# An attention and MLP kernel whose output split, normalising engine and early value loads were changed, together with one number of its planner

## The chip, the cores and the metric

One core of one Trainium2 chip. The metric is device microseconds of that core for one execution of the program. Ratios are computed as the mean time of one kernel's fast runs over the mean of the other's fast runs of the same rounds on the same chip, so they are not quite the ratios of the medians that are quoted.

## The reference

Eight batches of eight heads, 576 queries, 16 "beacon" keys in front of 576 ordinary ones, 64 wide; then an MLP over all 4,608 tokens.

```python
k_all = np.concatenate([beacon_k, k], axis=2)
v_all = np.concatenate([beacon_v, v], axis=2)
scores = np.matmul(q, k_all.transpose(0, 1, 3, 2)) / np.sqrt(D)   # causal for the ordinary keys
a = softmax(scores)
attn = np.matmul(a, v_all)                     # -> x [4608, 512]
h = x @ w_in                                   # 512 -> 2048
out = (h * sigmoid(1.702 * h)) @ w_out         # 2048 -> 512
```

## The kernel before

Attention runs in 32 steps (eight batches, four head pairs each). One step is: scores (TensorE, s<-qT,kT), exp (ScalarE, E<-s), masks on the diagonal blocks (GpSimd or VectorE, E<-E), outputs (TensorE, u<-E,vb), evictions (O<-u), and a normalisation on VectorE: two transposes that bring the sums of the exps together (zt<-O), a reciprocal, a transpose back (rz<-rt), two multiplications (xT<-O,rz). The MLP (u<-xT,w and u<-w,g) is cut into nine groups of 512 tokens and woven in between.

No instruction stands where a person put it. Each piece of work is an object with an estimated duration, an allowed engine or two, and a priority. A greedy planner runs once, while the program is built, and takes at each turn the piece that could start first by its estimates. The order that comes out is the fixed order of each engine's instructions.

```python
class Work:                     # eng: one engine with dur, or a dict of engines with their durations
    def __init__(self, eng, dur, key, fn, needs=(), alloc=None, dma=0.0, mode=0, after=()): ...
# --- cut ---
    zn.append(Work(
        "DVE", 0.68, i + 0.48, lambda i=i, x=x: z_turn(i, x), evs[-2:],   # 0.68 us: the estimate for zt<-O
        alloc=zb[0] if not zn else None, after=zn[:1],
    ))
# --- cut ---
    nw = Work(
        dict(DVE=0.78, POOL=1.42), 0, i + 0.45, lambda eng, i=i, x=x: norm(i, x, eng),
        [zk], alloc=xTb[b] if p + x == 0 else None, ...
    )
# --- cut ---
def issue():
    # --- cut ---
    # each turn: of all work whose needs are placed, the one with the smallest (start by estimate, mode, key)
    eng = min(w.opts, key=lambda e: max(t, free[e]) + w.opts[e] + ...)
    t = max(t, free[eng])
    c = (t, 0 if w.mode == mode == 1 else 1, w.key)
    # --- cut ---
order = issue()
for w in order:
    w.fn(w.eng) if w.flex else w.fn()
```

The outputs of a head are made in two parts of 288 queries, from nine matmuls. For batches 0 and 1 the values come in rows of 1,536 B and are spread to their partitions by matmuls with a constant matrix; from batch 2 on they are loaded straight to their rows.

```python
HS = S // 2
def av_list(x, half):
    qa, qe = half * HS, (half + 1) * HS
    return [(j, lo - qa, hi - qa, col) for j in range(NJ)
            for (lo, hi, col) in e_pieces(j, max(qa, s0s[j]), qe)]
# --- cut ---
def v_pe(b, j):                  # batches 0 and 1
    # --- cut: the beacons' values, by one matmul with the identity ---
    for t in range(TR):
        nc.tensor.matmul(u[:, :].rearrange("r (h d) -> r h d", h=H),
                         spread[:, j * P - t + TR : (j + 1) * P - t + TR], v6(b)[:, :, t, :], ...)
```

The softmax here doesn't subtract the row's maximum and nothing guards it: scores larger than these inputs give would overflow.

## Time and profile before

| | before |
|---|---|
| time, median of 7 runs beside the last experiments | 397.91 us |
| span of the profiled run | 395.7 us |
| TensorE, VectorE, GpSimd busy | 368.3, 259.0, 189.1 us |
| first MLP matmul | 47.49 us |
| four batch stages (exp table load to exp table load, 107.72 to 278.36 us) | 43.39, 41.80, 43.07, 42.38: 170.64 us |

ScalarE loads the exp table again after each group of gelus (seven loads of 1.28 us on the page), so these loads mark one batch's stage well, and two kernels can be compared stage by stage. The page's lines and the stage table are in the prediction. One more view was needed later: TensorE's own order in one of these stages (151.11 to 192.91 us; start, duration, what, how many; in brackets the wait in front and what ended it).

```profile
154.54 3.63 PE L512 MATMUL u<-w,g 128*128 128x512 f16 x16
158.10 0.60 PE L351 MATMUL s<-qT,kT 64*128 64x512 f16 x8
158.63 1.62 PE L421 MATMUL u<-E,vb 128*128 128x288 f16 x18
160.18 0.61 PE L351 MATMUL s<-qT,kT 64*128 64x464 f16 x4
160.72 3.63 PE L512 MATMUL u<-w,g 128*128 128x512 f16 x16
164.28 0.60 PE L351 MATMUL s<-qT,kT 64*128 64x512 f16 x8
164.81 1.62 PE L421 MATMUL u<-E,vb 128*128 128x288 f16 x18
166.36 0.37 PE L351 MATMUL s<-qT,kT 64*128 64x464 f16 x2
166.66 3.63 PE L512 MATMUL u<-w,g 128*128 128x512 f16 x16
170.22 0.48 PE L351 MATMUL s<-qT,kT 64*128 64x208 f16 x4
170.63 0.40 PE L421 MATMUL u<-E,vb 128*128 128x288 f16 x3
171.10 0.39 PE L351 MATMUL s<-qT,kT 64*128 64x64 f16 x6
172.01 0.37 PE L351 MATMUL s<-qT,kT 64*128 64x464 f16 x2 [0.53 <-ACT E L364]
172.32 0.54 PE L421 MATMUL u<-E,vb 128*128 128x224 f16 x4
174.19 1.01 PE L421 MATMUL u<-E,vb 128*128 128x208 f16 x11 [1.33 <-POOL E L387]
```

Twice there is a regular pattern: a w2 block of 16 matmuls (3.6 us), eight score matmuls, a whole step's 18 outputs, four score matmuls of 464 and 208 columns that feed the next step's last exps. The third time only two of those four stand in front of the w2 block. The other two come behind it, so that step's last exps and masks are no longer hidden under the block, the outputs are cut in pieces, and TensorE waits for a mask. I call this the broken third step.

### The profile page before, as it was taken

The numbers are of one execution on the slowest core, as the hardware profiler recorded it, in microseconds if no ns is written. First come the engines' busy times: TensorE is split into PE (matmuls) and PEld (weight loads), VectorE is DVE, ScalarE is ACT, GpSimd is POOL, SyncE is SP. The second block draws the span as 40 slices with busy tenths as digits, with TensorE's granted clock in tenths as the row PEclk, the third lists the DMA queues.
The fourth block names the chain that finished last, engine by engine and source line by source line (L and its number), as shares of the span: only waits on it lengthen the run. The fifth ranks groups of instructions, "written<-read, shape, count | busy, mean of one in ns | idle before, by whom it ended". The sixth has DMA issues, their size and how long they took to land.

```text
span 395.7 us, 6410 instructions
## 1 busy us (share of the span) xinstructions
PE 368.3 (93%) x2458; PEld 186.3 (47%) x2458; DVE 259.0 (65%) x425; ACT 227.3 (57%) x333; POOL 189.1 (48%) x282
## 2 busy tenths in 40 slices
PE   6997999989999799979997999979999999999996
PEld 3464544444544344534453774435454544444442
DVE  6469998699739973999469963997485349000021
ACT  1788766457674656656744766466658563644400
POOL 8664853469255854478337925584355044000000
PEclk9999999999999899999999899999999999999999
DMA  8999994849562795379346966279310010001022
GB/s 114 200 206 208 145 128 132 210 97 154 116 164 60 157 115 132 86 172 124 110 113 145 134 108 146 67 148 120 110 54 30 0 55 27 28 0 53 2 80 80
DMA packets 60894, 42.81 MB, mean 108 GB/s; under 512 B 32192, under 2 KB 53184, under 8 KB 60864
## 3 DMA queue, kind: packets, MB, share of 16 engines
q0 software_dynamic: 42816, 18.62, 38.8%
q1 hardware_dynamic: 18048, 23.79, 18.9%
q8 instruction: 19, 0.31, 0.3%
q14 instruction: 11, 0.09, 0.1%
HBM read 44.40 MB, written 16.61 MB: 154 GB/s over the span
## 4 chain that ended last, share of the span: by engine, by line
PE 50%; DVE 21%; DMA 5%; ACT 4%; issue 2%; POOL 2%; POOLq 1%; DVEq 0%; ACTq 0%
PE u L490 29%; PE u L512 13%; DMA n<-in_k_dram 5%; PE u L421 5%; DVE zt L444 4%; DVE O L432 4%; DVE xT L463 4%; DVE sq L275 4%; PE s L351 2%; ACT E L364 2%; ACT L364 2%; DVE rz L454 2%; DVE t L284 2%; POOL xT L463 1%; POOL t L284 1%
## 5 line engine op out<-in xcount | busy, mean ns | idle before, releaser
L490 PE MATMUL u<-xT,w 128*128 128x512 f16 (+1 forms) x640 | 133.7, 361 | 3.9 <-DVE O L432 1.6
L364 ACT ACTIVATE E<-s 128x1024 f16<-128x1024 f32 (+3 forms) x128 | 104.6, 873 | 49.2 <-PE s L351 45.5
L512 PE MATMUL u<-w,g 128*128 128x512 f16 x576 | 129.4, 379 | 2.3 <-DVE O L432 2.1
L502 ACT ACTIVATE g<-u 128x512 f16<-128x512 f32 x144 | 85.1, 597 | 59.6 <-PE u L490 59.3
L490 PEld LDWEIGHTS <-w 128*128 128x128 f16 x640 | 60.4, 99 | 62.7 <-issue 8.3
L512 PEld LDWEIGHTS <-g 128*128 128x128 f16 x576 | 54.8, 98 | 67.5 <-issue 3.4
L387 POOL TENSOR_SCALAR_AFFINE_SELECT E<-E 128x256 f16<-128x256 f16 (+2 forms) x144 | 58.6, 425 | 42.1 <-ACT E L364 40.8
L463 POOL TENSOR_TENSOR xT<-O,rz 64x576 f16<-64x576 f32 x24 | 40.8, 1701 | 71.6 <-DVE rz L454 71.5
L525 DVE COPY osb<-u 128x512 f32<-128x512 f32 x26 | 17.7, 681 | 76.9 <-PE u L512 76.8
L421 PE MATMUL u<-E,vb 128*128 128x288 f16 (+6 forms) x576 | 58.2, 246 | 7.8 <-POOL E L387 5.7
L432 DVE COPY O<-u 128x288 f32<-128x288 f32 x109 | 45.8, 442 | 27.0 <-PE u L421 26.5
L421 PEld LDWEIGHTS <-vb 128*128 128x128 f16 (+1 forms) x576 | 44.0, 98 | 25.6 <-issue 14.6
L444 DVE STREAM_TRANSPOSE zt<-O 64x576 f32<-64x576 f32 x64 | 49.4, 772 | 1.9
L463 DVE TENSOR_TENSOR xT<-O,rz 64x576 f16<-64x576 f32 x40 | 48.8, 1220 | 0.7
L351 PE MATMUL s<-qT,kT 64*128 64x80 f16 (+5 forms) x384 | 39.9, 286 | 6.1 <-ACT E L364 4.6
L284 POOL COPY t<-sq 128x576 f16<-128x576 f16 x22 | 30.7, 1397 | 26.6 <-DVE sq L275 26.6
L275 DVE STREAM_TRANSPOSE sq<-n 128x576 f16<-128x576 f16 x48 | 35.7, 755 | 4.4 <-DMA n<-in_k_dram 3.8
L351 PEld LDWEIGHTS <-kT 64*128 64x128 f16 x384 | 14.5, 94 | 32.6 <-issue 26.5
L454 DVE STREAM_TRANSPOSE rz<-rt 128x576 f32<-128x576 f32 x32 | 24.4, 762 | 1.3 <-DVE t L290 0.4
L243 POOL DMA_DIRECT2D vb<-in_v_dram x24 | 20.8, 873 | 0.0
L284 DVE COPY t<-sq 128x576 f16<-128x576 f16 x26 | 19.7, 757 | 0.5
L523 ACT COPY osb<-u 128x512 f32<-128x512 f32 x10 | 5.9, 588 | 17.0 <-PE u L512 17.0
(50 smaller groups left out, 147.0 us busy)
## 6 DMA issues: line engine op xcount, KB each, us to landing
out_dram<-osb SPq DMA_DIRECT2D x36, 256.0 KB
d<-t SPq DMA_DIRECT2D x24, 148.0 KB
kT<-d SPq DMA_DIRECT2D x12, 296.0 KB
n<-in_k_dram POOLq DMA_DIRECT2D x12, 288.0 KB, 5.3
n<-in_q_dram POOLq DMA_DIRECT2D x12, 288.0 KB, 6.2
d<-t SPq DMA_DIRECT2D x24, 144.0 KB
qT<-d SPq DMA_DIRECT2D x12, 288.0 KB
vb<-in_v_dram POOLq DMA_DIRECT2D x18, 128.0 KB, 5.5
```

Of the source, the lines that this page charges most:

```text
L275: nc.vector.transpose(sqs[(b, g, w)][:, c * n : (c + 1) * n, :, :], nat[(b, g, w)][:, c * n : (c + 1) * n, :],)
L284: copy[eng](out=tqk[(b, g, w)][:, e, o : o + S].rearrange("p (r t) -> p r t", t=TPP), in_=sqs[(b, g, w)][:, :, e, :].rearrange("p t r -> p ...
L351: nc.tensor.matmul(sc[:, x, o : o + e - a], kT[r : r + 64, p, j * P : (j + 1) * P], qT[r : r + 64, p, a:e], start=True, stop=True,)
L364: nc.scalar.activation(out=Es[i][:, :, choff[ci] : choff[ci] + w], in_=scs[(i, ci)][:, :, 0:w], func=AFT.Exp, scale=0.125,)
L387: nc.gpsimd.affine_select(out=blk, in_=blk, compare_op=ALU.is_ge, fill=0.0, base=mc, pattern=[[0, 2], [1, w]], channel_multiplier=-1,)
L421: nc.tensor.matmul(u[:, lo:hi], vb[0:kw, j, :, :].rearrange("r h c -> r (h c)")[:, o : o + 2 * D], E[0:kw, x, col : col + hi - lo], start= ...
L432: copy[eng](out=Os[i][:, x, half * HS : (half + 1) * HS], in_=avu[(i, x, half)][:, :])
L444: nc.vector.transpose(zst[i][0][64 * x : 64 * x + 64, :, :], Os[i][64 * (1 - x) : 64 * (1 - x) + 64, x, :])
L463: vec[eng].tensor_tensor(out=xT[r : r + 64, p, c : c + S], in0=Os[i][r : r + 64, x, :], in1=zst[i][2][r : r + 64, :], op=ALU.mult,)
L490: nc.tensor.matmul(u[:, o : o + w], w1t[:, kp, nt * P : (nt + 1) * P], xT[:, kp, m : m + w], start=(kp == 0), stop=(kp == NKP - 1),)
L502: nc.scalar.activation(out=gts[g][:, nt, :], in_=hu[(g, nt)][:, :], func=AFT.Gelu_apprx_sigmoid)
L512: nc.tensor.matmul(o[:, :], gts[g][:, nt, mt * P : (mt + 1) * P], w2t[:, nt, :], start=(nt == 0), stop=(nt == NNT - 1),)
```

## The change

Its stated intent: split the outputs at query 240, where a key block begins, and merge neighbouring pieces (seven matmuls a head for nine); normalise on VectorE only; load the second batch's values straight to their rows, behind w1. With that come an earlier mask constant, the second weight placed behind the next q and k, per-batch buffer names, and one planner estimate: 0.68 became 0.74.

```diff
-    HS = S // 2
+    HS = 2 * P - Nb
+    AQ = (0, HS, S)
+    NBV = 1
 # --- cut: u tile and evictions by AQ ---
-            if lo < hi:
+            if lo < hi and got and got[-1][1] == lo and got[-1][2] + lo - got[-1][0] == col + lo - qa:
+                got[-1] = (got[-1][0], hi, got[-1][2])
+            elif lo < hi:
                 got.append((lo, hi, col + lo - qa))
 # --- cut: rings qT0, qT1, kT0, kT1, vb0, vb1 of one buffer each for qT, kT, vb of two ---
-    mkeep = Work("POOL", 0.3, 0.0, make_keep)
+    mkeep = Work("POOL", 0.3, -4.75, make_keep)
 # --- cut: spread matmuls only for b < NBV; bk loads no longer wait for batch 1's values ---
-                "POOL", 0.9 + 0.6 * (j == 0), 4 * b - 1.5 + 0.1 * j,
+                "POOL", 0.9 + 0.6 * (j == 0), (4 * b - 1.5 if b >= NB2 else -3.9) + 0.1 * j,
                 lambda b=b, j=j: load_v(b, j, 0, H),
-            [vpe[NJ - 1], vpe[2 * NJ - 1]][c > 0 :][:1] if c < 3 else [], dma=3.0,
+            vpe[-1:] if 2 * c < 3 * NBV else [], dma=3.0,
+            after=[Lq[(2, 1, 0)]],
-                "DVE", 0.68, i + 0.48, lambda i=i, x=x: z_turn(i, x), evs[-2:],
+                "DVE", 0.74, i + 0.48, lambda i=i, x=x: z_turn(i, x), evs[-2:],
-                dict(DVE=0.78, POOL=1.42), 0, i + 0.45, lambda eng, i=i, x=x: norm(i, x, eng),
+                dict(DVE=0.78), 0, i + 0.45, lambda eng, i=i, x=x: norm(i, x, eng),
```

More of the change, by code (lines that the diff above doesn't have):

```diff
@@ L81 @@
     bkn = cst.tile([Nb, NB2, H, D], F16, tag="bkn", name="bkn")
-    bvn = cst.tile([Nb, NB2, H, D], F16, tag="bvn", name="bvn")
+    bvn = cst.tile([Nb, NBV, H, D], F16, tag="bvn", name="bvn")
     def make_keep():
@@ L166, in load_beacons @@
             out=t.rearrange("n b h d -> n (b h) d"),
-            in_=src[0:NB2].rearrange("b h n d -> n (b h) d"),
+            in_=src[0 : t.shape[1]].rearrange("b h n d -> n (b h) d"),
         )
@@ L401, in av_list @@
     def av_list(x, half):
-        qa, qe = half * HS, (half + 1) * HS
+        qa, qe = AQ[half : half + 2]
         return [
@@ L413, in av_half @@
         E = Es[i]
-        u = psu.tile([P, HS], F32, tag="u", name="u")
+        u = psu.tile([P, AQ[half + 1] - AQ[half]], F32, tag="u", name="u")
         avu[(i, x, half)] = u
@@ L432, in av_out @@
         copy[eng](
-            out=Os[i][:, x, half * HS : (half + 1) * HS], in_=avu[(i, x, half)][:, :]
+            out=Os[i][:, x, AQ[half] : AQ[half + 1]], in_=avu[(i, x, half)][:, :]
         )
@@ L552 @@
     rings = dict(
-        n0=2, n1=2, sq=2, t0=2, t1=2, d0=4, d1=4, qT=2, kT=2, vb=2, s=2, E=2, u=4, O=3,
+        n0=2, n1=2, sq=2, t0=2, t1=2, d0=4, d1=4, qT0=1, qT1=1, kT0=1, kT1=1, vb0=1, vb1=1, s=2, E=2, u=4, O=3,
         zt=2, rt=2, rz=2, xT=RING, g=2, osb=3,
@@ L586, in first_loads @@
                     ))
-        lv = Work("POOL", 0.8, kl + 0.2, lambda b=b: load_v6(b), dma=3.6)
-        fb = []
         ub = Buf("u")
@@ L610, in first_loads, with first_values @@
         pk[b] = y
+    def first_values(b):
+        lv = Work("POOL", 0.8, -4.8, lambda b=b: load_v6(b), dma=3.6)
         for j in range(NJ):
@@ L613, in first_loads @@
             kk = 4 * b + 0.5
-            x = Work("PE", 1.35, kk, lambda b=b, j=j: v_pe(b, j), [lv, mspread] + beac[1:], alloc=ub, after=vpe[-1:])
+            x = Work("PE", 1.35, kk, lambda b=b, j=j: v_pe(b, j), [lv, mspread] + beac[1:], alloc=ub,
+                after=vpe[-1:],
+            )
             V[(b, j)] = Work(
@@ L624 @@
     for b in range(B):
-        kTb[b], qTb[b], vbb[b], xTb[b] = Buf("kT"), Buf("qT"), Buf("vb"), Buf("xT")
+        kTb[b], qTb[b], vbb[b] = (Buf(f"{n}{b % 2}") for n in ("kT", "qT", "vb"))
+        xTb[b] = Buf("xT")
         bt = [qTb[b], kTb[b]]
@@ L628 @@
             first_loads(b)
-            continue
-        for g in range(2):
+        for g in range(2) if b >= NB2 else ():
             for w in (1, 0):
@@ L659 @@
                         bkB = [
-                            Work("POOL", 0.6, 4.3, lambda x=x: load_bk(x), [V[1, 0]], dma=0.7)
+                            Work("POOL", 0.6, 4.3, lambda x=x: load_bk(x), after=[ld_], dma=0.7)
                             for x in range(HG)
@@ L681 @@
                 placed[(b, g, w)] = pl
+        if b < NBV:
+            first_values(b)
+            continue
         for j in range(NJ):
             V[(b, j)] = Work(
-                "POOL", 0.9 + 0.6 * (j == 0), 4 * b - 1.5 + 0.1 * j,
+                "POOL", 0.9 + 0.6 * (j == 0), (4 * b - 1.5 if b >= NB2 else -3.9) + 0.1 * j,
                 lambda b=b, j=j: load_v(b, j, 0, H),
```

## The prediction

> **What bounds the kernel now.** I read the page's busy table first, then the chain that ended last, then one table of busy time by stage (cut at the moments where a gelu group begins or ends), then TensorE's own waits, and last the engines' order of instructions in the first 65 us and from 107 to 135 us.
>
> The page's first part, busy us and share of the span, and its line of the chain by engine:
>
> ```profile
> PE 368.3 (93%) x2458; PEld 186.3 (47%) x2458; DVE 259.0 (65%) x425; ACT 227.3 (57%) x333; POOL 189.1 (48%) x282
> ...
> PE 50%; DVE 21%; DMA 5%; ACT 4%; issue 2%; POOL 2%; POOLq 1%; DVEq 0%; ACTq 0%
> ```
>
> TensorE is busy 93% and carries half of the chain. VectorE carries 21% though it is busy only 65%, so it binds in some stages. By stage (span of the stage, then busy us of TensorE, its weight loads, VectorE, ScalarE and GpSimd, each with its number of instructions, then granted clock, DMA share, GB/s):
>
> ```profile
> 22.97:47.49 24.52, 21.65 (x233) 12.83 (x229) 23.31 (x40) 20.16 (x34) 15.82 (x33) 1.00 1.23 188
> 47.49:107.00 59.51, 55.64 (x367) 27.44 (x364) 52.30 (x85) 36.82 (x55) 32.81 (x42) 1.00 0.78 138
> 107.00:151.00 44.00, 41.05 (x253) 19.89 (x252) 33.61 (x56) 26.71 (x38) 25.03 (x35) 0.96 0.65 125
> 151.00:193.00 42.00, 39.41 (x251) 19.05 (x250) 33.18 (x55) 26.41 (x39) 25.02 (x35) 1.00 0.69 131
> 193.00:236.00 43.00, 40.60 (x313) 25.92 (x312) 32.91 (x54) 26.17 (x38) 25.02 (x35) 0.96 0.65 118
> 236.00:278.00 42.00, 38.88 (x248) 18.88 (x247) 32.58 (x54) 25.86 (x37) 25.01 (x35) 1.00 0.67 123
> 278.00:335.00 57.00, 56.75 (x363) 28.11 (x362) 34.17 (x60) 35.15 (x50) 22.35 (x36) 1.00 0.13 46
> 335.00:395.70 60.70, 55.62 (x257) 24.94 (x255) 6.84 (x10) 19.11 (x32) 1.90 (x1) 0.99 0.11 39
> ```
>
> From the first value (22.97 us, first attention output) to the first MLP matmul (47.49 us) VectorE is busy 23.31 of 24.52 us: that stage is VectorE's. The four batch stages of 42 to 44 us are TensorE's, with 2.4 to 3.1 us of gaps each. In two of them the clock is 0.96: 0.04 x 43 us is another 1.7 us each. From 278 us on there is almost nothing to win but one wait of 1.2 us for a GpSimd normalisation. The pool of lost TensorE time from 47 us to 278 us is so 3.9 + 2.95 + 2.6 + 2.4 + 3.1 + 2 x 1.7, about 18 us.
>
> Two groups that the change touches (busy us, mean ns):
>
> ```profile
> L463 DVE TENSOR_TENSOR xT<-O,rz 64x576 f16<-64x576 f32 x40 | 48.8, 1220 | 0.7
> L463 POOL TENSOR_TENSOR xT<-O,rz 64x576 f16<-64x576 f32 x24 | 40.8, 1701 | 71.6 <-DVE rz L454 71.5
> L214 PE MATMUL u<-w,spread 96*128 96x512 f16 x60 | 13.5, 380 | 0.0
> ```
>
> And what a batch stage's gap hangs on (GpSimd's order, start and duration):
>
> ```profile
> 108.83 1.90 POOL L463 TENSOR_TENSOR xT<-O,rz 64x576 f16<-64x576 f32 x1 [5.51 <-DVE rz L454]
> 110.81 0.38 POOL L387 TENSOR_SCALAR_AFFINE_SELECT E<-E 128x224 f16<-128x224 f16 x1
> 111.13 0.62 POOL L131 DMA_DIRECT2D n<-in_k_dram  x1
> ```
>
> GpSimd sat 5.51 us in front of a normalisation, and the mask and the next k load queued behind it. VectorE's transposes of that k began only at 116.98 us, after 1.48 us of waiting for it, and from there VectorE was full to 144 us, with a TensorE gap of 1.46 us at 130.3.
>
> [...]the normalisation has two SBUF inputs, takes 719 ns at best and up to 2519 ns on VectorE, and its mean is 1220 ns while GpSimd does 24 of the 64. [...]The trace has 18 attention matmuls with 3,328 columns[...] in 1.55 us[...]. [...]A row of v is 64 values, 256 B in HBM, and the page lists 32192 of 60894 packets under 512 B[...]. [...]here a gap of 1.46 us at 130 us already went with a granted clock of 0.67 over 130 to 135 us[...].
>
> **The change part by part.**
>
> *Split at 240.* Per head the pieces were 288, 176, 48 and 224, 64, 288, 288, 208, 80: nine. Key blocks begin at queries 0, 112, 240, 368 and 496, and the block at 240 no longer reaches into the first part; the 224 and 64 lie side by side and merge. New: 240, 128 and 336, 336, 336, 208, 80: seven, with the same 1,664 columns. 128 matmuls and weight loads go. [...]I take 0.8 us. Evictions keep their columns. The first part now needs only two masks, which helps latency.
>
> *Second batch's values.* Goes: 30 matmuls at 216 ns and one with the identity, 6.7 us of TensorE (it ran 36.97 to 44.4 us), four evictions of 0.58 us on ScalarE and one of 0.69 us on VectorE, and one 576 KB load. Comes: six loads, issues of 0.55, 0.84 and 4 x 0.90 us, 5.0 us of GpSimd; the same bytes in 256 B rows. Elsewhere such a batch of v was issued at 90.3 to 96.1 us and the queues calmed at about 100 us, so about 10 us of the queue, against 3 us (0.59 MB written at the 200 GB/s of this stage): 7 us more, in a stage where DMA is busy until 57 us. The 6.7 us are not all won, since VectorE binds there: from 23.9 us to the last normalisation of the first batch at 44.03 us it has hardly a gap. TensorE is held up by the removed work only from there to 47.49 us. So the MLP can start at about 44 us, 3.5 us sooner; if the values land too late for step 4's output to have run before it, 1.6 us of that is only postponed. I take 2.5 us.
>
> *Early mask constant, second weight behind the next q and k.* The constant was ready at 18.2 us, with VectorE waiting 4.5 us for it; now VectorE can mask the first steps while GpSimd issues loads. No gain in itself, since the first output waits for the first batch's values until 22.2 us; it protects against the longer GpSimd queue.
>
> *Normalising on VectorE.* GpSimd loses 40.8 us. VectorE gains 24 instructions. Without a partner two in a row took 1.49 to 1.63 us (28.8 to 42.5 us), 0.78 each; with some blocking by GpSimd's remaining copies I take 0.85: 64 x 0.85 = 54.4 against 48.8, +5.6 us. GpSimd, being freer, will take some of VectorE's 26 reordering copies (0.757 us each); six of them give 4.5 us back. VectorE's sum hardly changes. What is won is order: masks and k loads no longer stand behind a normalisation. At 110 us the k load could go 0.6 us sooner, and VectorE could begin up to 1.2 us sooner. A quarter of the 18 us pool, with the clock, is 4.5 us; the wait of 1.2 us near the end shrinks by 0.4. I take 4.6 us for both.
>
> *Buffer names* change only the order of allocation. Sum: 0.8 + 2.5 + 4.6 = 7.9 us; 397.88 - 7.9 = 390.0 us.
>
> **The rivals.** (a) TensorE's sum is all that counts: 6.7 + 0.8 us come off, and the gaps shrink too. For it: 93% busy, MLP work can fill any gap. Against: the removed 6.7 us lie in VectorE's stage. It gives 386 us. (b) The new loads hurt. GpSimd's ninth open load waited for the first to land: issue 10 waited for 2, issue 15 for 7, issue 16 for 8. If eight may be open, the last value loads wait for w1, whose issues take 16.7 us to land, and the masks behind them wait until about 28 us; the second weight, last issued at 46.9 us before and needed at 65.9, could land late as well and open a gap before the second MLP matmul. That gives back 3 to 5 us: 393 to 395. (c) VectorE becomes the bound in the batch stages: they hold 33 of 42 us of it. With 5.6 us spread over eight batches and bursts already full, gaps grow by 0.5 us each: 394 us. (d) Nothing in the middle moves, because k loads are gated by an exp (109.01 to 110.04 us) and not by the normalisation; then 397.88 - 3.3 = 394.6 us.
>
> **Range and chances.** Line of 2%: 389.9 us, just where I land. (a) and a fuller start pull down to 384, (b) to (d) up to 396. The schedule is rebuilt as a whole from estimates, so a step may miss by a few us either way. Faster by over 2%: 0.47; within 2%: 0.49; slower: 0.04.
>
> **What would show it.** The identity and spread matmuls number 31, not 62; attention matmuls 448; GpSimd has no normalisation and the 64 on VectorE average 0.75 to 0.95 us. The first MLP matmul starts at 43 to 45.5 us; if it is at 47 or later, the start's step is wrong. Gaps and lost clock from there to the end of the last batch stage fall from about 18 to about 13 us; if they stay, (d) holds, and if they grow with VectorE full, (c). A gap before the first w2 matmul, or masks in the first 30 us held up behind value loads, shows (b). A kernel at 386 or below would say that removed TensorE work counts in full.

## The result, and the profile after

The changed kernel takes 386.65 us (385.37 to 387.29, four runs) against 397.99; the ratio is 0.9706, 95% interval 0.9671 to 0.9741: faster. The time lies inside the predicted range of 384 to 396 us, 3.35 us below its estimate of 390.0. The stages tell another story than the prediction's sum, though.

| stage | before | after | difference |
|---|---|---|---|
| to the first MLP matmul | 47.49 | 51.21 | +3.72 |
| first gelu group (to 65.97 / 67.27) | 18.48 | 16.06 | -2.42 |
| first stage (to 107.72 / 109.41) | 41.75 | 42.14 | +0.39 |
| four batch stages | 170.64 | 157.82 | -12.82 |
| the rest | 117.34 | 116.37 | -0.97 |
| span | 395.7 | 383.6 | -12.1 |

The start got worse, where 2.5 us were to be won. The four batch stages gave all the gain, in columns as in the prediction's stage table:

```profile
109.41:149.29 39.88, 38.91 (x233) 18.52 (x232) 33.54 (x57) 25.90 (x37) 19.22 (x32) 1.00 0.72 138
149.29:188.52 39.23, 38.88 (x234) 18.43 (x232) 33.59 (x58) 25.79 (x37) 18.82 (x32) 1.00 0.74 135
188.52:228.00 39.48, 39.04 (x297) 24.73 (x296) 33.21 (x58) 25.82 (x37) 19.33 (x32) 1.00 0.76 135
228.00:267.23 39.23, 38.88 (x233) 18.41 (x232) 33.60 (x58) 25.79 (x37) 18.75 (x32) 1.00 0.75 134
```

TensorE is busy 38.9 of 39.2 us and the clock is 1.00: a stage without gaps. GpSimd has 6 us less, VectorE no less than before. The normalisation group, all on VectorE now:

```profile
L467 DVE TENSOR_TENSOR xT<-O,rz 64x576 f16<-64x576 f32 x64 | 52.2, 816 | 0.9
```

The start has lines that answer to the prediction's rival (b). GpSimd's order (start, duration, what, and the wait in front):

```profile
23.93 0.88 POOL L245 DMA_DIRECT2D vb<-in_v_dram  x1 [1.68 <-DMA w<-in_moe_w_in_dram]
26.43 0.73 POOL L245 DMA_DIRECT2D vb<-in_v_dram  x1 [1.62 <-DMA w<-in_moe_w_in_dram]
27.16 1.73 POOL L391 TENSOR_SCALAR_AFFINE_SELECT E<-E 128x256 f16<-128x256 f16 x5
```

TensorE's order at the same place:

```profile
28.26 2.73 PE L425 MATMUL u<-E,vb 128*128 128x128 f16 x13 [3.46 <-POOL E L391]
```

Two stretches of 2 us, with the granted clock third from the end:

```profile
26.00:28.00 2.00, 0.00 (x0) 0.00 (x0) 0.00 (x0) 0.00 (x0) 1.57 (x4) 0.73 1.24 206
36.00:38.00 2.00, 2.00 (x11) 0.87 (x10) 1.97 (x4) 1.84 (x4) 2.00 (x4) 0.50 1.09 158
```

The last value loads wait for w1 to land, the masks of step 1 stand behind them, TensorE stands still for 3.46 us, and its clock is then at half (0.50) until about 41 us. That is rival (b), and dearer than it was priced.

The first stage has one more gap, in front of the first w2 matmul. The two score matmuls there stand behind an exp for which ScalarE first finishes its gelus (the last starts at 66.65 us) and loads a table (1.28 us from 67.27 us):

```profile
69.64 0.37 PE L355 MATMUL s<-qT,kT 64*128 64x464 f16 x2 [3.02 <-ACT E L368]
69.94 3.63 PE L516 MATMUL u<-w,g 128*128 128x512 f16 x16
```

The second weight is not what is late: its four loads, issued from 43.1 us on, took 14.4 us at most to land. This gap of 3.02 us is in the traces of all six kernels below that have the values' part, and in none of the other eight.

### The profile page after: what moved, and what is told of

It is laid out like the page before. It is cut to its first block, busy times and chain, and to the rows that moved or that the text cites.

```text
span 383.6 us, 6063 instructions
## 1 busy us (share of the span) xinstructions
PE 363.8 (95%) x2299; PEld 180.3 (47%) x2299; DVE 264.4 (69%) x446; ACT 226.2 (59%) x334; POOL 149.0 (39%) x260
## 4 chain that ended last, share of the span: by engine, by line
PE 69%; DMA 11%; ACT 8%; DVE 7%; issue 2%; POOL 2%; SPq 0%; ACTq 0%; POOLq 0%; DVEq 0%
PE u L494 28%; PE u L516 24%; PE u L425 11%; PE s L355 6%; ACT E L368 5%; DMA w<-in_moe_w_in_dram 4%; DMA d<-t 3%; ACT L368 2%; DVE zt L448 2%; DVE O L436 2%; DMA n<-in_k_dram 2%; DVE xT L467 1%; DMA g<-in_q_dram 1%; DMA qT<-d 1%; DVE sq L277 1%
## 5 line engine op out<-in xcount | busy, mean ns | idle before, releaser
L506 ACT ACTIVATE g<-u 128x512 f16<-128x512 f32 x144 | 83.8, 598 | 51.4 <-PE u L494 51.2
L529 DVE COPY osb<-u 128x512 f32<-128x512 f32 x29 | 19.6, 675 | 76.1 <-PE u L516 76.0
L425 PE MATMUL u<-E,vb 128*128 128x336 f16 (+4 forms) x448 | 59.4, 277 | 3.5 <-POOL E L391 3.5
L436 DVE COPY O<-u 128x240 f32<-128x240 f32 (+1 forms) x103 | 42.4, 432 | 20.1 <-PE u L425 18.6
L467 DVE TENSOR_TENSOR xT<-O,rz 64x576 f16<-64x576 f32 x64 | 52.2, 816 | 0.9
L425 PEld LDWEIGHTS <-vb 128*128 128x128 f16 (+1 forms) x448 | 39.7, 101 | 26.0 <-issue 9.0
L355 PE MATMUL s<-qT,kT 64*128 64x80 f16 (+5 forms) x384 | 40.8, 293 | 7.5 <-ACT E L368 6.3
L286 POOL COPY t<-sq 128x576 f16<-128x576 f16 x24 | 28.7, 1196 | 32.3 <-DVE sq L277 31.8
L286 DVE COPY t<-sq 128x576 f16<-128x576 f16 x24 | 26.6, 1108 | 0.2
L245 POOL DMA_DIRECT2D vb<-in_v_dram x28 | 24.5, 881 | 5.7 <-DMA w<-in_moe_w_in_dram 3.3
L436 ACT COPY O<-u 128x336 f32<-128x336 f32 (+1 forms) x25 | 10.3, 428 | 7.7 <-PE u L425 7.7
```

The source lines that it names most:

```text
L286: copy[eng](out=tqk[(b, g, w)][:, e, o : o + S].rearrange("p (r t) -> p r t", t=TPP), in_=sqs[(b, g, w)][:, :, e, :].rearrange("p t r -> p ...
L355: nc.tensor.matmul(sc[:, x, o : o + e - a], kT[r : r + 64, p, j * P : (j + 1) * P], qT[r : r + 64, p, a:e], start=True, stop=True,)
L425: nc.tensor.matmul(u[:, lo:hi], vb[0:kw, j, :, :].rearrange("r h c -> r (h c)")[:, o : o + 2 * D], E[0:kw, x, col : col + hi - lo], start= ...
L436: copy[eng](out=Os[i][:, x, AQ[half] : AQ[half + 1]], in_=avu[(i, x, half)][:, :])
L467: vec[eng].tensor_tensor(out=xT[r : r + 64, p, c : c + S], in0=Os[i][r : r + 64, x, :], in1=zst[i][2][r : r + 64, :], op=ALU.mult,)
L506: nc.scalar.activation(out=gts[g][:, nt, :], in_=hu[(g, nt)][:, :], func=AFT.Gelu_apprx_sigmoid)
```

## The experiments

The questions: which part removes the gaps of the batch stages, and what delays the start? Twelve kernels ran, all correct. The columns "figure" to "values" say what of the change a kernel has; "stages" is the sum of the four batch stages, "rest" the span from the first MLP matmul on.

| run | figure | norm. on VectorE | split 240 | values | first MLP | stages | rest | ratio to before |
|---|---|---|---|---|---|---|---|---|
| before | 0.68 | | | | 47.49 | 170.64 | 348.2 | 1 |
| b1_norm_dve | 0.68 | yes | | | 47.74 | 164.85 | 343.9 | 0.9927 |
| b2_norm_flip | 0.68 | in place | | | 47.60 | 165.45 | 342.1 | 0.9849 |
| b3_split240 | 0.68 | | yes | | 47.52 | 169.39 | 345.1 | 0.9921 |
| b4_values | 0.68 | | | yes | 51.89 | 167.91 | 347.6 | 1.0085 |
| c1_norm_split | 0.68 | yes | yes | | 47.97 | 164.40 | 341.6 | 0.9853 |
| e2_after_z68 | 0.68 | yes | yes | yes | 52.67 | 166.84 | 343.5 | 1.0030 |
| e1_z_only | 0.74 | | | | 49.63 | 158.82 | 334.2 | 0.9692 |
| c2_norm_split_z | 0.74 | yes | yes | | 47.09 | 158.02 | 332.5 | 0.9615 |
| c3_norm_values | 0.74 | yes | | yes | 50.15 | 158.82 | 337.1 | 0.9752 |
| the changed kernel | 0.74 | yes | yes | yes | 51.21 | 157.82 | 332.4 | 0.9706 |
| d1_late_values | 0.74 | yes | yes | later | 48.97 | 157.53 | 332.1 | 0.9669 |
| d2_later_values | 0.74 | yes | yes | later still | 49.20 | 157.08 | 335.8 | 0.9743 |
| e3_z78 | 0.78 | yes | yes | | 48.80 | 158.67 | 334.3 | 0.9646 |

**The parts one by one.** My theory after the result was that GpSimd's queue had been in the way and the normalisations' move had cleared it. The rivals were the split and the values.

b1_norm_dve, normalisations on VectorE alone:

```diff
-                dict(DVE=0.78, POOL=1.42), 0, i + 0.45, ...
+                dict(DVE=0.78), 0, i + 0.45, ...
```

> The kernel before with one edit: normalisations may only go to VectorE (the plan is made anew). Theory N (the batch stages are gap-free in the changed kernel because GpSimd's in-order queue no longer stands behind a normalisation): the four stages from one exp table load to the next between 107 and 278 us fall from 43.4, 41.8, 43.1, 42.4 us to 40 to 41 us (the changed kernel has 39.9, 39.2, 39.5, 39.2), the clock is 1.00 in them, and the whole takes 0.97 to 0.98 of before (386 to 391 us); the start is unchanged. Rival S (the split at 240 does it): ratio 0.995 to 1.005 and the stages stay at 42 to 43. Rival V (the values' new load shifts the plan): as S.

Measured: 0.9927 (0.9895 to 0.9959), stages of 41.2 us each. The stages lost 5.8 us of 170.6, not 12.8, and the first stage grew from 41.75 to 44.70 us, so the whole moved only 0.7%. The theory holds for less than half of the gain.

b2_norm_flip keeps the plan of the kernel before in every place and only issues the 24 GpSimd normalisations on VectorE:

```diff
-        w.fn(w.eng) if w.flex else w.fn()
+        w.fn("DVE" if 1.42 in w.opts.values() else w.eng) if w.flex else w.fn()
```

> The kernel before with its plan kept in every place: the order is the one computed with both engines allowed, but each of the 24 normalisations planned for GpSimd is issued on VectorE at its place. Theory N says it is GpSimd's queue and not a new plan: stages of 40 to 41.5 us, ratio 0.97 to 0.985. If only the new plan helps, ratio 0.99 to 1.01.

Measured: 0.9849 (0.982 to 0.9879), at the edge of theory N's range, with stages of 40.8 to 42.2 us, two of them above its 41.5. The same move with the old order is worth 1.5%, with a newly computed plan 0.7%. So replanning itself moves the time by as much as a part of the change does.

b3_split240, the split and the merging alone:

```diff
-    HS = S // 2
+    HS = 2 * P - Nb
+    AQ = (0, HS, S)            # and the merging of pieces, as in the change
```

> The kernel before with only the split at query 240 and the merged pieces. Theory N: attention matmuls 448 for 576, about 1 us off: ratio 0.995 to 1.0, stages 41.5 to 43. Rival S: stages 39.5 to 40.5 us, ratio 0.97 to 0.98.

Measured: 0.9921 (0.9889 to 0.9953), a little more than expected; 1.3 us of it in the first stage (40.42 for 41.75 us) and as much in the four batch stages together. Rival S is out: the batch stages stay at about 42 us.

b4_values has the change with its normalisation, split and figure undone:

```diff
 # the changed kernel, with
-    HS = 2 * P - Nb
+    HS = S // 2                # and no merging
-                "DVE", 0.74, i + 0.48, ...
+                "DVE", 0.68, i + 0.48, ...
-                dict(DVE=0.78), 0, i + 0.45, ...
+                dict(DVE=0.78, POOL=1.42), 0, i + 0.45, ...
```

> The kernel before with only the part for the second batch's values (their loads, the order of the weight loads and the masks' constant, the buffers' names). Theory: the first MLP matmul comes later than 47.5 us, at about 51, because mask instructions stand behind value loads that wait for w1; TensorE loses 6.7 us of work; ratio 0.99 to 1.01. Rival V: the batch stages fall to 40 us and the ratio is 0.975 to 0.985.

Measured: 1.0085 (1.0051 to 1.0118), slower, though within 2%; first MLP matmul at 51.89 us, as expected. The batch stages stay at 41.7 to 42.3 us, so rival V is out. Taking 31 matmuls off TensorE, with all that came with it, made the kernel slower. No part alone comes near 0.9706, and their effects taken together (-0.7 or -1.5, -0.8 and +0.9%) would give -0.6 to -1.4%.

**The parts together.** c1_norm_split joins b1 and b3; c2_norm_split_z is c1 with one number changed:

```diff
-                "DVE", 0.68, i + 0.48, lambda i=i, x=x: z_turn(i, x), evs[-2:],
+                "DVE", 0.74, i + 0.48, lambda i=i, x=x: z_turn(i, x), evs[-2:],
```

> The kernel before with two parts: normalisation on VectorE only, and the split at 240 with merged pieces; the second batch's values stay as they were. Alone the two gave 0.993 and 0.992. Theory P (only both together leave the batch stages without gaps: with the normalisations moved alone, TensorE still waited 8.2 us for output evictions on VectorE): stages of 39.2 to 39.8 us, first MLP matmul at 47.5 us, ratio 0.962 to 0.970, so faster than the changed kernel, whose start is 4 us later. Rival A (the parts just add): ratio 0.985, stages of 40.5 us, and the values' part is needed for the rest.

> As the run before it, and with the plan's figure for the sum's transpose at 0.74 instead of 0.68 us, as in the changed kernel. Theory P: within 0.3% of the run before it, stages 39.2 to 39.8 us. Rival Z (that planning figure is what removes the gaps): this one 0.962 to 0.970 and the run before it 0.98 or more.

Measured: c1 0.9853 (0.981 to 0.9896) with stages of 41.1 us, c2 0.9615 (0.9566 to 0.9664) with three stages of 39.2 us and one of 40.3. Theory P fell and rival Z, which I had put in only because the line stood in the diff, won. (c1's ratio is also that of rival A, by which the parts just add; but A needs the values' part for the rest of the gain, and c2 has the rest without it.) An estimate of a duration was worth 2.4%, and c2 at 382.28 us is the fastest kernel measured; its interval just misses the changed kernel's (0.9671 to 0.9741), which was measured in other rounds. TensorE's waits in c1 and in c2 (in total us, times, longest):

```profile
PE u L493 <- DVE O L435: 7.7, 5, 1.6
```

```profile
PE u L493 <- DVE O L435: 0.9, 5, 0.3
```

The evictions in front of the MLP matmuls came in time in c2, though the instructions are nearly the same ones and VectorE is busy no less (264.37 for 263.48 us).

c3_norm_values is the changed kernel with the split undone (`HS = S // 2`, no merging).

> The changed kernel with the split put back to 288 and the pieces unmerged (normalisation and values' part kept). Theory P: the gaps of the batch stages come back to 41 us each, first MLP matmul at 51 us, ratio 0.990 to 1.0. If the values' part is what interacts with the normalisation, ratio 0.97 to 0.975.

Measured: 0.9752 (0.9703 to 0.9802), stages of 39.2 to 40.3 us: theory P fell here too. The other half of the expectation names a cause, values with normalisation, that is not needed either, as e1 shows below. The changed kernel, with the split, is 0.5% faster (0.9752 against 0.9706, intervals overlapping), mainly in the first stage (45.20 against 42.14 us). That difference is one of clock: behind the same gap of 3.02 us the w2 block of 16 matmuls took 6.34 us here and 3.63 us in the changed kernel, and the clock of the first stage was 0.92 here and 1.00 there. So it is not shown to be the split's.

d1_late_values asks about the start: the second batch's value loads wait, in the plan, for step 1's first exp, so that four masks come before them.

```diff
+    for j in range(NJ):
+        late.append((V[(1, j)], 1))
```

> The changed kernel, but in the plan the second batch's value loads wait for the first exp of step 1, so that four of that step's mask instructions stand in front of them on GpSimd. Theory M (the late start of the MLP comes from masks behind loads that may not be issued until w1 has landed): the gap of 3.46 us before 28.26 us goes, the second step's output runs at about 25 us, the first MLP matmul comes at 46.5 to 49 us for 51.2, and the ratio to before is 0.960 to 0.967 (0.9706 without it). Rival D (the data itself, 256 B rows in a full queue, comes late): first MLP matmul stays at 50 us or later and the ratio at 0.970 or above.

Measured: 0.9669 (0.962 to 0.9717), first MLP matmul at 48.97 us; the wait of 3.46 us became two of 1.33 and 1.57. This agrees with theory M, but the interval overlaps the changed kernel's.

**The figure.** e1_z_only changes nothing in the kernel before but 0.68 to 0.74; e2_after_z68 puts 0.68 back in the changed kernel.

> The kernel before with one number changed: the planner's duration for the sum's transpose is 0.74 us for 0.68 (the trace has 0.772). No instruction is added or taken away, only the order may differ. Theory Z (this figure is the main part of the gain by itself): ratio 0.97 to 0.98, batch stages 39.5 to 41 us. Theory NZ (it needs the normalisations on VectorE, as a plan in which both fit): ratio 0.99 to 1.005, stages 42 us.

> The changed kernel with only that number put back to 0.68. Both Z and NZ: the batch stages go back to about 41 us each, ratio to before 0.985 to 0.995 (0.9706 with 0.74). If the stages stay at 39.2 us, the figure mattered only without the values' part.

Measured: e1 0.9692 (0.9645 to 0.974), e2 1.003 (0.9973 to 1.0088). The number alone gives what the whole change gives, and the whole change without it gives nothing; e2 is slower than either theory had expected, since what its batch stages gain (3.8 us) its start loses (5.2 us). e1 still has 24 normalisations on GpSimd, nine matmuls a head and the spread values, and three of its stages take 39.29 us. The first of them, in the stage table's columns:

```profile
107.69:146.98 39.29, 38.72 (x249) 19.01 (x248) 32.86 (x58) 25.52 (x36) 22.81 (x33) 1.00 0.73 136
```

And TensorE's order in its second stage:

```profile
162.24 0.60 PE L351 MATMUL s<-qT,kT 64*128 64x464 f16 x4
162.77 3.63 PE L512 MATMUL u<-w,g 128*128 128x512 f16 x16
166.33 0.60 PE L351 MATMUL s<-qT,kT 64*128 64x512 f16 x8
166.86 1.62 PE L421 MATMUL u<-E,vb 128*128 128x288 f16 x18
```

In front of the third w2 block there are now four score matmuls for the two of before, and the third step's 18 outputs run whole, without a wait. The traces show the same in all four batch stages of all fourteen kernels of the table: with 0.68 (seven kernels, 28 stages) the third step is always broken in this way, and with 0.74 or 0.78 (seven kernels, 28 stages) it is always whole. With a broken step the normalisations' place matters (42.7 us a stage before, 41.2 in b1, as means of the four); with a whole one it does not (39.7 in e1 and in c3). Of the 2.51 us by which the kernel before's second stage is longer than e1's, 2.03 us are gaps of TensorE (2.59 for 0.56), and 1.86 us of these stand inside the broken step (0.53 and 1.33).

ScalarE's order shows where the plans part. Kernel before, second stage:

```profile
164.39 0.59 ACT L523 COPY osb<-u 128x512 f32<-128x512 f32 x1 [2.45 <-PE u L512]
164.87 2.85 ACT L364 ACTIVATE E<-s 128x1024 f16<-128x1024 f32 x3
170.53 3.13 ACT L364 ACTIVATE E<-s 128x416 f16<-128x416 f32 x4 [2.81 <-PE s L351]
```

e1:

```profile
160.64 3.36 ACT L364 ACTIVATE E<-s 128x1024 f16<-128x1024 f32 x4 [2.82 <-POOL t L284]
```

With 0.68 the output of the w2 block (osb<-u) is copied by ScalarE in front of the third step's exps, of which only three run before the next block; with 0.74 VectorE copies it and all four run. This choice of engine, too, goes with the figure in all 56 stages. The reason can be read off the planner, which needs no chip; run alone on the kernel before with each figure, it gives these estimates (not measurements). With 0.68 VectorE finishes a reciprocal 0.02 us before that output is ready and takes two transposes first, so the copy goes to ScalarE and the exps start 0.24 us later. The last two score matmuls need a score buffer that the second of these exps frees, and so could start 0.15 us after TensorE is free. A greedy planner does not wait 0.15 us: it puts the w2 block of 3.46 us in front of them. With 0.74 the reciprocal ends later, the output is taken first, by VectorE, and the score matmuls are in time.

e3_z78 asks if a figure nearer the truth is what helps; the trace's mean is 0.772 us.

```diff
 # c2_norm_split_z, with
-                "DVE", 0.74, i + 0.48, ...
+                "DVE", 0.78, i + 0.48, ...
```

> The best version so far (normalisation on VectorE, split at 240, old values, ratio 0.9615) with the figure at 0.78, near the measured 0.772, for 0.74. If a figure near the truth is what helps: stages 39.2 to 39.5 us, ratio 0.958 to 0.966. If 0.74 is a lucky number of this greedy planner: stages of 40.5 us or more, ratio above 0.97.

Measured: 0.9646 (0.9596 to 0.9696), stages of 39.6 to 39.8 us: the step is whole, the stages a little longer than c2's. So 0.74 is no needle's eye. The planner alone, for the kernel before, breaks the third step in all four stages at 0.68, in three at 0.69 and in none from 0.70 to 0.74.

d2_later_values puts the value loads behind step 2's first exp (`late.append((V[(1, j)], 2))`).

> As the run with later value loads, but they wait in the plan for the first exp of step 2, so that all mask instructions of step 1 stand in front of them. Theory M: the first MLP matmul, 51.2 us in the changed kernel and 49.0 with the loads behind step 1's first exp, comes at 46 to 48 us, ratio 0.958 to 0.965. Rival D (late data): 49 us or later, ratio 0.966 or more.

Measured: 0.9743 (0.9687 to 0.9798), first MLP matmul at 49.20 us. TensorE waited for no mask in the start any more, and yet the MLP began no sooner than in d1: between 20 and 50 us it waited 4.3 us for exps and 2.0 us for a copy of q on VectorE. Theory M as the whole explanation fell. The masks held behind the loads are one wait of the changed kernel's start, and where they go others take their place; rival D's numbers fit, but late data was not seen to be the cause either. What sets the start is open: it lay between 47.1 and 52.7 us, with e1 at 49.63 although e1 changes no load, only the order. That d2 is slower than d1 as a whole is not the start's doing: its first stage took 45.59 for 42.17 us, at a clock of 0.93 for 1.00.

## Why the prediction was right or wrong

The range and the sign were right, 386.65 us in 384 to 396, though "within 2%" had been given a little more chance (0.49) than "faster" (0.47). That the sum came out near was luck: two of its errors offset each other (a start 3.7 us later for 2.5 us won, and 12.8 us in the batch stages for 4.6 us there and near the end), and the term that decided was missing.

**What bounds the kernel.** Right for the batch stages: TensorE binds (38.9 to 39.0 us busy of 39.2 to 39.9 in the changed kernel), and 18 us lay in gaps and lost clock between 47 and 278 us. Reckoned as there, 5.3 us of gaps are left in the changed kernel from 51.2 to 267.2 us, where about 13 us had been forecast. That VectorE binds the start was not tested. What the gaps hang on was read wrongly: the gap of 1.46 us at 130.3 us was put down to a k load behind a normalisation on GpSimd, but it ended with a mask, in the broken third step. In e1's second stage GpSimd still waits 5.62 us and normalises for 1.90 us in front of a k load (at 149.88 us), and TensorE's gaps of the stage are 0.56 us in all.

**Split at 240.** Counts right (448 matmuls, seven a head). 0.8 us was taken, an estimate; alone it gave 0.8%, about 3 us, 1.3 us of that in the first stage, with a new plan as part of it. The effect of the matmuls alone was not isolated.

**Second batch's values.** A failed step, with the wrong sign: "TensorE is held up by the removed work only from there to 47.49 us. So the MLP can start at about 44 us, 3.5 us sooner". It started 3.7 us later. Rival (b) had its first half, waits of GpSimd loads for earlier ones (1.68 and 1.62 us) with masks behind them, just as the trace has it; its size left out the clock, at 0.50 for some 12 us behind a wait of 3.46. The sign of the second half, a gap before the first w2 matmul, was there too (3.02 us), but for another reason than a late weight: it ended with an exp. Alone the part makes the kernel slower (1.0085), and at 0.74 the kernel without it is faster (0.9615 against 0.9706).

**Early mask constant.** No run has it alone. VectorE does step 0's masks (11.96 to 16.0 us) while GpSimd issues loads, as predicted, but step 1's masks stood behind the value loads all the same.

**Normalising on VectorE.** The durations were right: 816 ns a piece for the predicted 850 (780 measured before, the other 70 the author's estimate), 52.2 us for 54.4 (in the kernel before two in a row took 2.52 to 2.55 us beside a GpSimd copy of 1.67 to 1.70 us, and single ones 1.41 to 2.52 us when they started while GpSimd normalised; but the share alone does not give the 1220 ns of before: in e1, with the 24 still on GpSimd, VectorE's 40 take 898 ns each), GpSimd down by 40.1 us. That "VectorE's sum hardly changes" was wrong: it rose by 5.4 us, for GpSimd took over two of the reordering copies instead of six, and VectorE's other 24 took 1108 ns each for 757. The sentence that failed is "A quarter of the 18 us pool, with the clock, is 4.5 us". The stages gave 12.8 us. For what the normalisation's move does by itself in them (5.8 us in b1, 5.2 us in b2) 4.5 us is near. (With 0.4 us near the end that made 4.9; 4.6 was taken, without a reason given.) The rest of the 12.8 us came from a line of the diff that the prediction never priced: the planner's 0.68 made 0.74. I read it as bookkeeping, since it adds no instruction. It is the main cause of the gain, by e1 and e2.

**Signs set in advance.** "A kernel at 386 or below would say that removed TensorE work counts in full": it came to 386.65, and b4 shows that reading would have been wrong. A total can land where a theory puts it for another reason. Rivals (c) and (d) are out: VectorE's sum grew about as (c) said, but the gaps shrank.

**What is shown and what is argued.** Shown: the figure alone carries the gain (e1, e2, and c2 against c1). Since e1 does the same work as the kernel before, the order, with the choice of engines, is the whole cause. The broken third step goes with the figure in all fourteen kernels. Argued from the traces: that of all that differs in the order it is this step that makes the longer stages; no run changed TensorE's order there and nothing else. Not shown: that the normalisation and the split add anything to the figure (c2's 0.9615 against e1's 0.9692, intervals overlapping).

## What to carry to other kernels

Where a planner computes the instruction order from estimated durations, an estimate is part of the kernel: a change of one number can outweigh every change of instructions, so separate it with a run of its own, and judge any part both with its new plan and in the old order. A greedy planner may place a long block to avoid a very short wait; a plan can be searched for that without a chip. A gain found for a bundle belongs to no member of it before each is taken out and put in alone; here the fastest kernel measured leaves out one of the stated parts. Compare stage by stage before believing a total that agrees with the forecast.

## What the traces show of the clock, the loads and the gaps

- In these traces the clock did not follow the length of the gap alone. In the kernel before, a gap of 1.46 us at 130.3 us was followed by a clock of 0.50 over 132 to 135 us, while one of 1.33 us in the next stage was not (1.00 over 172 to 178 us). After the changed kernel's wait of 3.46 us the clock stayed at 0.50 from 28 to 40 us and was 1.00 from 41 to 46 us, with TensorE, while it was 0.50, busy 1.7 to 2.0 of every 2 us by the profile. Behind the same gap of 3.02 us the w2 block took 6.34 us in c3_norm_values and 3.63 us in the changed kernel.
- The changed kernel's value loads at 23.93 and 26.43 us, the 20th and 21st from GpSimd, waited 1.68 and 1.62 us for the 12th and 13th, parts of w1, to land. What sets this was not tested.
- TensorE's repeated gaps of 2.4 to 3.1 us in each batch stage shrank to 0.6 us in three of four stages with no buffer changed, by another order alone (e1_z_only), though in the plan it was a score buffer not yet free that tipped the order.
